# A four-layer linear/softmax attention kernel: side work of the first linear passes planned by steps, weights' preparation loosened, residuals and the attention's first rows asked for elsewhere

## The chip, the cores and the metric

The kernel runs on one core of one Trainium2 chip. The metric is the device time of one execution in microseconds; three runs are shown, and their median counts. One further execution was taken by the hardware profiler; all rows of the profile come from it.

## The reference, cut to what matters

Input x has 2048 rows of 512; 32 heads of 16. Four layers follow one another, A, B, A, B, each reading the layer norm of x and adding its result to x. Both A layers share their weights, and so do both B layers.

```
def _A_ref(x, wqkv, w_phi, wo):                # linear attention with a learned feature map
    q, k, v = split_heads(x @ wqkv)
    pq, pk = q @ w_phi, k @ w_phi              # per head, 16 x 16
    phi_q = concat(softmax(pq), softmax(-pq))  # 32 features a head
    phi_k = concat(softmax(pk), softmax(-pk))
    kv, z = phi_k^T v, sum over rows of phi_k
    o = phi_q kv / (phi_q z + 1e-6)
    return heads_joined(o) @ wo

def _B_ref(x, wq, wk, wv, wo, beta):           # 4 segments of 512 rows, causal softmax within each
    for s in range(4):
        a_dot = softmax(qs ks^T / 4 + mask) vs
        a_mem = phi(qs) M / (phi(qs) z + 1e-6)         # phi(t) = t + 1 if t > 0, else exp(t)
        out_s = sigmoid(beta) * a_mem + (1 - sigmoid(beta)) * a_dot
        M, z = M + phi(ks)^T vs, z + sum phi(ks)
    return joined(out) @ wo

x = x + _A_ref(layernorm(x), ...)
x = x + _B_ref(layernorm(x), ...)
x = x + _A_ref(layernorm(x), ...)
x = x + _B_ref(layernorm(x), ...)
```

## The kernel before, in words

**Tiles.** The 2048 rows are 16 tiles of 128 (`NT`) in four segments of four. A 512-wide weight is held as high and low part (`hi`, `lo`), and each projection of a tile is twelve matmuls of 128x512 (`mm3`: four chunks, three products each), made by a generator that yields after each three. All projections, transposes and sums share three PSUM buffers `g`; the key-value sums use `lg` and `mx`.

**Layer A, first pass** (`pass1`). It goes over the segments in the order `SEGS` = 1, 2, 3, 0. In each, `go` runs the steps k0 k1 q0 q1 k2 v0 k3 q2 q3: a k step projects a key tile (`kproj`), copies it on ACT, takes each head's extremes on DVE (`extremes`) and their differences on POOL (`differences`); `exp` on ACT and `scale_k` (sums on DVE, one half multiplied on DVE, one on POOL) follow one and two steps later. A q step projects a query tile (`qproj`), copies it, takes its extremes, and stores it to DRAM (`pqs`). Step v0 is `kv(0)`, the sum of keys times values over the first two tiles; `kv(1)`, over the last two, is put into the next segment as `late`, behind k0. Each yield of `go` is one step i; a segment has 34 to 36. Beside them, from i = 4 on, one step of a chain of generators `side` is made per i: first the last four steps of the next segment's norm (`columns`: transposes into `hT`), then `v_tile` for the next segment (16 steps), then eleven steps (`rows`) of the norm after that (`norm_T` with `slow`: load of four tiles; four steps of statistics on DVE; `root` on ACT; `refine` on POOL; four steps of `normal` on ACT). What is left of `side` at the segment's end is stepped through alone. The first segment of the second A layer has all four parts in `side`, since there the pass begins within the end of layer B.

**Weights' preparation** (`prepare`). In the first A layer it is run turn by turn with `pass1`: one yield of each. It loads B's and A's other weights in blocks, splits each piece into `hi` (a cast on ACT, tile `oh`) and `lo` (a subtraction on POOL, tile `ol`), and stores both to DRAM: 32 pieces of a quarter block for `wqk`, then twelve whole 128x512 pieces. There are three buffers each of `xr` (the load), `oh` and `ol`. One piece is taken every `EVERY` = 2 yields, after `PREP` = 6 more.

**The order on each engine.** A scheduler places the instructions, but each helper engine (`dve`, `act`, `pool`, `sync`) is wrapped in `Ordered`: every instruction is chained behind the one issued before it on its engine, so that program order holds there. `held` does the same for PE. A list put off until the end of layer B, `aside`, takes the work of the next pass's first key tiles (`features`) out of the way of B's last sums.

**Layer A, second pass** (`pass2`). For each tile i: transposes of its features (8), their product with the key-value sums (16 small matmuls), normalisation, transposes of the result of tile i - 1 (`turn`), and `out_proj` of tile i - 1 with its residual, which `residual` loads and `end` adds on DVE and stores. The residual of tile i is asked for after `out_proj` of tile i - 1. A tile is nine steps. The first `A20` = 82 steps run alone, but for the `opening` of layer B, which is stepped at some of them (two loads of `wqk`, four of `bwv`, eleven steps of the first segment's norm, four `fills` of constants). The rest is done within B's loop.

**Layer B** (`steps`). A loop over slots k from `BEGIN` = -31 runs the attention by a table; heads come in groups m, five slots each: `maxima` (products, then row maxima on DVE; slot 5m - 9 on, tile `mx`), `attend` (tile `lg`, exponentials on ACT, masks on POOL; slot 5m on), `weighted` (`pv`). `BEFORE` lists what the slots below zero do: at -30 to -27 the `columns` of the first segment (`ln0`), from -25 on the projections. The rest of pass 2 is spread over slots -9 to 1 by its PE work: each slot brings the total up to its share of `LEFT` = 40000 ns, and the last does what remains. The slots after that follow tables that the change does not touch, and at the end of the first B layer they step through the second A layer's `pass1` (`after`).

Of the kernel before, what the change touches and what calls it, by code (L numbers as in the profile page):

```python
# [34 lines left out]
LEAD = 9  # L35
FINAT = 8
PAUSE, DONE = object(), object()
LEFT = 40000
BEGIN = -31
MAXIMA = -9  # L40
A20 = 82
PREP = 6
EVERY = 2
NEXT = (3, 2, 3, 2)
SEGS = (1, 2, 3, 0)
# [51 lines left out]
6.1 max out~       | 6.3 fin           | 6.4 pt~  # L97
7.1 p pt~          | 7.3 fin p pt      | 7.4 p pt
"""
BEFORE = {-30: "ln0", -29: "ln0", -28: "ln0", -27: "ln0", -25: "q0", -23: "v0", -21: "k0", -20: "load", -19: "v1",  # L100
          -18: "n", -17: "v2 n", -16: "n", -15: "n n", -14: "q1 n", -13: "n", -12: "k1 n", -11: "n", -10: "v3 n",
          -4: "max q2~", -1: "t0"}

# [2 lines left out]
def interleave_kernel(ctx, tc, x_in, a_wqkv, a_wphi, a_wo, b_wq, b_wk, b_wv, b_wo, b_beta,  # L106
# [24 lines left out]

    last = [None]
    ends = {}
    put_off = [None]
    aside = [None]

# [12 lines left out]

    class Ordered:  # L150

        def __init__(self, engine):
            self.engine = engine

        def __getattr__(self, op):
            f = getattr(self.engine, op)

            def call(*a, **k):
                i = f(*a, **k)  # L159
                if self.engine in ends:  # L160
                    behind(i, ends[self.engine])
                ends[self.engine] = i
                return i
            return call

# [32 lines left out]
    def constants():  # L198

        sync.dma_start(out=mask, in_=c_mask)  # L200
        sync.dma_start(out=eb, in_=b_beta.unsqueeze(0).broadcast_to([P, H]))
        yield
        act.activation(eb, eb, AF.Exp, scale=-1.0)
        dve.tensor_scalar(eb, eb, 1.0, None, op0=ADD)
        dve.reciprocal(gates[:, 1, :], eb)
        dve.tensor_scalar(gates[:, 0, :], gates[:, 1, :], -1.0, 1.0, op0=MUL, op1=ADD)
        for j in range(4):
            dve.tensor_copy(share[32 * j : 32 * j + 32, :], gates[32 * j : 32 * j + 32, 0, j:H:4])
        dve.tensor_scalar(share, share, -1.0, bd[:, 24:25], op0=ADD, op1=MUL)
        dve.tensor_scalar(share, share, 1.0, None, op0=ADD)  # L210
        dve.tensor_copy(ones, bd[0:32, 25:26].broadcast_to([32, P]))
# [84 lines left out]
    def prepare():  # L296


        yield from constants()
        for _ in range(PREP):  # L300
            yield
        jobs = [(src, kc) for src in (b_wq, b_wk, a_wo, b_wv, b_wo) for kc in range(NC)]
        asked = []

        def rows():

            while jobs and len(asked) < 3:
                src, kc = jobs.pop(0)
                asked.append(T2("xr", 3))
                sync.dma_start(out=asked[-1], in_=src[kc * P : (kc + 1) * P, :])  # L310
            return asked.pop(0)

        def parts():
            return rows(), T2("oh", OO, F32R), T2("ol", OO, F32R)

        def pieces():
            for m in range(2):
                for kc in range(NC):
                    tiles = parts()
# [12 lines left out]

        copied, stored = None, None
        for piece in chain(pieces(), (None, None)):
            if stored:
                _, keep, tiles = stored
                for k, t in zip(keep, tiles):
                    dma(k, t.rearrange("p (c x) -> p c x", c=NC) if len(k.shape) == 3 else t)
            if copied:
                (raw, hi, lo), _, _ = copied  # L340
                pool.tensor_tensor(out=lo, in0=raw, in1=hi.bitcast(F32), op=SUB)
            if piece:
                (raw, hi, _), _, _ = piece
                act.copy(hi, raw)
            copied, stored = piece, copied
            for _ in range(EVERY):
                yield
# [166 lines left out]
    def chain(*gens):  # L514
        for g in gens:
            yield from g
# [56 lines left out]
    class LayerA:  # L573
# [68 lines left out]
        def pass1(self, first):  # L642
# [5 lines left out]
                spare = ("e8" if first else "w8") if n % 2 else None  # L648
                return h, norm_T(self.xsrc, SEGS[n], h, spare, slow=True, off=True)

            def rows(g):
                for _ in range(11):
                    next(g)
                    yield

            if first:
                wq, wk, wv, upc = self.first(hTs, vv, upcoming)
            else:
# [16 lines left out]
            for n, s in enumerate(SEGS):  # L675
# [55 lines left out]
                if n < NSEG - 1:  # L731
                    if n == 0 and not first:
                        upc = upcoming(1)
                        next(upc[1])
                    hTs, g = upc
                    vv = []
                    side = [] if n or first else [rows(g)]
                    side += [g, v_tile(hTs, wv, vv, ("g", G))]
                    if n + 2 < NSEG:
                        upc = upcoming(n + 2)  # L740
                        side.append(rows(upc[1]))
                    side = chain(*side)
                    e = {}

                    def go(late):

                        ready, done = [], []
                        for step in "k0 k1 q0 q1 k2 v0 k3 q2 q3".split():
                            if step == "v0":
                                yield from kv(0)  # L750
                                continue
                            t = int(step[1])
                            yield from (kproj if step[0] == "k" else qproj)(t, e)
                            if done:
                                es.append(scale_k(e[done.pop()]))
                            if ready:
                                exp(e[ready[0]])
                                done.append(ready.pop())
                            if step[0] == "k":
                                ready.append(t)  # L760
                            if step == "k0" and late:
                                yield from late

                    for i, _ in enumerate(go(late)):
                        if i == 4 and n == 0 and not first:
                            wq = load_w("awq", None, "e8")
                        if aside[0] is None and i > 3:
                            next(side, None)
                        if n == 1 and i % 4 == 0:
                            settle(1)  # L770
                        yield
                    for _ in side:
                        yield
                    late = kv(1)
                    continue

# [35 lines left out]
        def pass2(self):  # L812
# [4 lines left out]
            for i in range(NT + 1):  # L817
# [15 lines left out]
                if i < NT:  # L833
# [13 lines left out]
                    if i + 3 < NT:  # L847
                        self.e[i + 3] = differences(*self.raw.pop(i + 3))
                    self.load_q(i + 4)
                if i > 0:  # L850
                    yield from out_proj(x, self.xdst, i - 1, oT, self.wo)
                if i < NT:
                    x = residual(self.xsrc, i, ("ot", OT))


    class LayerB:
# [271 lines left out]
        def opening(self):  # L1128
            self.w4 = []
            self.wnext = [(m, c) for _ in range(NSEG) for c in range(NC) for m in range(2)]  # L1130
            for _ in range(2):
                self.queue_w()
                yield
            self.wv = []
            yield from bring(self.wv, "bwv")
            self.norm0 = self.norm(0)
            next(self.norm0)
            fills = self.start()
            for n in (0, 0, 1, 1, 1, 1, 1, 1, 0, 1, 1, 1, 1):
                yield  # L1140
                next(fills, None)
                for _ in range(n):
                    next(self.norm0)

        def steps(self, side, after, table_end):

# [134 lines left out]
    for i in range(2):  # L1281
# [3 lines left out]
        opening = lb.opening()  # L1285
        for k in range(A20):
            next(a2)
            if k % 3 == 0 and (5 < k < 24 or k > 41):
                next(opening, None)
        for _ in opening:  # L1290
            pass
# [32 lines left out]
```

## Time and profile before

| | us |
|---|---|
| median of three runs | 1654.8 |
| runs | 1653.51, 1654.8, 1656.23 |
| profiled execution, own time | 1648.24 |
| its span, first to last instruction | 1646.1 |
| mean granted TensorE clock | 0.972 |

In the profile PE is TensorE's matmuls, PEld its weight loads, DVE VectorE, ACT ScalarE, POOL GpSimd, SP the queue that issues the DMAs. A row of a wait reads: who waited, for whom, total us, times, longest. A row of a stretch reads: from and to, length, then busy us and instructions of PE, PEld, DVE, ACT and POOL, the granted clock, the DMA engines' share and GB/s. A row of a timeline reads: start, duration, engine, operation, written tile and read tiles, size, number; in brackets the idle time before it and what ended that. L159 and L180 are the helpers through which nearly all instructions go, so tiles tell them apart: `tb` is the copy of a query tile, `U` of a key tile, `P` the features, `x` rows being normalised, `st` their statistics, `oh` and `ol` the parts of a prepared weight (or of a turned result), `xr` and `ot` residuals (`xr` also a weight's load).

The stages of the span: the first A layer's first pass until about 235 us, its second pass until 296 with a rest until 381, B until about 850 with the second A layer's start inside, the second A layer's first pass until about 1038, its second pass until 1098 with a rest until 1183, and B.

### The profile page before, as it was taken

The page shows a single profiled execution, that of the slowest core. Times are in us where ns is not written, and L with a number is a line of the kernel's source. Part 1 is how long each engine was busy: PE and PEld are TensorE (multiplying, and loading weights), DVE is VectorE, ACT ScalarE, POOL GpSimd, SP SyncE. Part 2 cuts the span into 40 slices and gives each one's busy share as a digit, 9 for nine tenths or more (in the row PEclk, how much of TensorE's full clock was granted, in tenths as well). Part 3 has the DMA queues.
Part 4 walks back from the last instruction along what each step waited for, and adds up shares of the span by engine and source line. Part 5 has one row for each costly group of instructions (what it writes and reads, how often), then busy time and mean ns, then how long its engine had stood idle before and what let it go on. Part 6 is the DMA issues. An engine that isn't in the chain of part 4 may idle for free.

```text
span 1646.1 us, 28161 instructions
## 1 busy us (share of the span) xinstructions
PE 1532.6 (93%) x9856; PEld 1095.2 (67%) x9856; DVE 1130.5 (69%) x3252; ACT 787.4 (48%) x1178; POOL 652.4 (40%) x1006
## 2 busy tenths in 40 slices
PE   7978899998899999999998989999889999999998
PEld 6766687775566666666567778877656666666554
DVE  5544377486887877888644456666777778777784
ACT  5334334434656556556532333344355655654553
POOL 1445474322444444433222235543134445533422
PEclk9978999999999999999997989999999999999999
DMA  4265537434533533534241102455344444343331
GB/s 157 84 230 159 177 99 220 147 114 116 169 97 97 155 94 106 144 97 109 89 164 45 39 26 65 157 156 174 113 127 123 117 116 134 86 135 92 91 76 60
DMA packets 108763, 195.69 MB, mean 119 GB/s; under 512 B 14416, under 2 KB 27856, under 8 KB 107856
## 3 DMA queue, kind: packets, MB, share of 16 engines
q1 hardware_dynamic: 107472, 193.38, 39.9%
q8 instruction: 79, 1.29, 0.3%
q10 hardware_dynamic: 1152, 0.52, 0.1%
q14 instruction: 60, 0.49, 0.1%
HBM read 101.05 MB, written 39.85 MB: 86 GB/s over the span
## 4 chain that ended last, share of the span: by engine, by line
PE 64%; DVE 19%; issue 5%; ACT 5%; POOL 3%; DMA 2%; SPq 1%; ACTq 0%; POOLq 0%; DVEq 0%
PE g L180 36%; DVE mx L159 8%; PE mx L180 8%; PE lg L180 7%; PE pv L180 6%; PE g L184 6%; POOL P L159 2%; DVE es L159 2%; ACT P L159 2%; ACT tb L159 2%; DVE mxs L159 1%; DVE bs L159 1%; DVE mmq L159 1%; DVE ta L159 1%; DMA ot<-in 1%
## 5 line engine op out<-in xcount | busy, mean ns | idle before, releaser
L159 DVE CUSTOM_DVE_ANT_0 mx<-mx,mask 128x128 f32<-128x128 f32 (+3 forms) x1024 | 510.9, 499 | 163.7 <-PE mx L180 129.2
L159 ACT ACTIVATE P<-lg 128x1024 f32<-128x1024 f32 x320 | 328.8, 1028 | 185.4 <-PE lg L180 173.1
L159 POOL TENSOR_SCALAR_AFFINE_SELECT P<-P 128x256 f32<-128x256 f32 (+1 forms) x448 | 191.3, 442 | 438.2 <-ACT P L159 436.8
L180 PE MATMUL g<-hh,wqk 128*128 128x512 f32 x512 | 182.5, 411 | 2.4 <-ACT hh L159 1.7
L180 PE MATMUL mx<-e,e 63*128 63x256 f32 (+2 forms) x1024 | 155.6, 361 | 23.0 <-DVE mxs L159 17.2
L180 PE MATMUL lg<-e,e 64*128 64x256 f32 (+2 forms) x1024 | 168.7, 387 | 8.0 <-ACT P L159 7.1
L180 PE MATMUL g<-w,oh 128*128 128x512 f32 x512 | 168.4, 410 | 2.5 <-ACT oh L159 2.1
L180 PE MATMUL pv<-P,v 128*32 128x512 f32 (+3 forms) x2048 | 164.9, 441 | 0.0
L180 PEld LDWEIGHTS lg<-e,e 64*128 64x128 f32 x1024 | 81.4, 185 | 103.8 <-issue 53.6
L180 PE MATMUL g<-w,hh 128*128 128x512 f32 x448 | 146.6, 408 | 1.2 <-ACT tb L159 0.9
L159 DVE DVE_READ_ACCUMULATOR2_ANT mxs<- 128x1 f32 x1024 | 144.9, 142 | 0.0
L180 PEld LDWEIGHTS mx<-e,e 63*128 63x128 f32 x1024 | 83.5, 186 | 71.2 <-DVE mxs L159 52.3
L180 PEld LDWEIGHTS pv<-P,v 128*32 128x32 f32 x2048 | 53.6, 109 | 98.2 <-issue 88.2
L180 PEld LDWEIGHTS g<-hh,wqk 128*128 128x128 f32 x512 | 98.2, 192 | 24.3 <-ACT hh L159 2.1
L180 PEld LDWEIGHTS g<-w,oh 128*128 128x128 f32 x512 | 89.2, 188 | 23.9 <-ACT oh L159 3.5
L159 POOL TENSOR_SCALAR tb<-tb 128x512 f32<-128x512 f32 x48 | 71.5, 1491 | 84.2 <-ACT tb L159 84.2
L180 PE MATMUL g<-w,ol 128*128 128x512 f32 x256 | 101.3, 396 | 1.4 <-DVE ol L159 1.4
L180 PE MATMUL g<-hl,wqk 128*128 128x512 f32 x256 | 101.7, 397 | 0.2
L159 ACT CAST ta<-g 128x512 fp32r<-128x512 f32 x64 | 37.5, 585 | 122.1 <-PE g L180 122.1
L180 PEld LDWEIGHTS g<-w,hh 128*128 128x128 f32 x448 | 79.7, 190 | 20.4 <-ACT tb L159 3.1
L159 DVE TENSOR_REDUCE mmq<-tb 128x32 f32<-128x512 f32 x64 | 40.9, 680 | 72.1 <-ACT tb L159 72.1
L159 POOL TENSOR_TENSOR P<-P,es 128x512 f32<-128x512 f32 x32 | 49.1, 1533 | 102.4 <-DVE es L159 102.1
(133 smaller groups left out, 2794.3 us busy)
## 6 DMA issues: line engine op xcount, KB each, us to landing
e<-ta SPq DMA_DIRECT2D x384, 128.0 KB
wqk<-wqk SPq DMA_DIRECT2D x64, 512.0 KB
x<-x SPq DMA_DIRECT2D x48, 256.0 KB
xr<-in SPq DMA_DIRECT2D x28, 256.0 KB
pq<-tb SPq DMA_DIRECT2D x24, 256.0 KB
tb<-pq SPq DMA_DIRECT2D x24, 256.0 KB
x<-xr SPq DMA_DIRECT2D x24, 256.0 KB
xr<-x SPq DMA_DIRECT2D x24, 256.0 KB
```

The costliest lines, as they stand in the source:

```text
L159: i = f(*a, **k)
L180: return held(nc.tensor.matmul(*a, **k))
L184: return held(nc.tensor.transpose(*a))
```

## The change

Constants: `LEFT` 40000 to 25000, `BEGIN` -31 to -25, `A20` 82 to 105, `PREP` 6 to 3 (with one more yield within `constants`).

In `pass1` the chain `side` is replaced by `plan`, a list of pairs of a step and a generator: at step i every entry due is made. In the ordinary segments `columns` stay at steps 4 to 7, the sixteen steps of `v_tile` lie from 10 to 34, and the eleven of the later norm at 8, 14, 16, 18, 20, 22, 24, 28, 30, 32, 34, among them. In the second A layer's first segment the first norm's remaining steps lie at 8 to 20, four of them (the statistics) being appended to `aside`; `v_tile` lies from 21 to 33, and the later norm from 21 to 36. What is due after the end is made without yields. `late` goes behind k1 instead of k0.

`Ordered` gets a flag `loose`: instructions issued under it are still placed behind the last chained one of their engine, but later ones are not chained behind them. `prepare` issues all its casts, subtractions, loads and stores under it.

In `pass2` the residual of tile i is asked for before `out_proj` of tile i - 1. The `opening` has the whole norm of the first segment, fifteen steps with its `columns`, spread with the `fills` over steps of pass 2, and `BEFORE` loses its four `ln0`.

```
-LEFT = 40000
-BEGIN = -31
+LEFT = 25000
+BEGIN = -25
-A20 = 82
-PREP = 6
+A20 = 105
+PREP = 3
-BEFORE = {-30: "ln0", -29: "ln0", -28: "ln0", -27: "ln0", -25: "q0", ...
+BEFORE = {-25: "q0", ...
...
                 if self.engine in ends:
                     behind(i, ends[self.engine])
-                ends[self.engine] = i
+                if not loose[0]:
+                    ends[self.engine] = i
...  # prepare
-        copied, stored = None, None
-        for piece in chain(pieces(), (None, None)):
+        def turn_by_turn():
+            loose[0] = True
+            piece = next(todo, None)
+            loose[0] = False
+            return piece
+
+        copied, stored, todo = None, None, pieces()
+        for piece in chain(iter(turn_by_turn, None), (None, None)):
+            loose[0] = True
             if stored:
...
+            loose[0] = False
             copied, stored = piece, copied
             for _ in range(EVERY):
                 yield
...  # pass1
-                    side = [] if n or first else [rows(g)]
-                    side += [g, v_tile(hTs, wv, vv, ("g", G))]
+                    if n or first:
+                        plan = [(4 + j, g) for j in range(4)]
+                        vals, norms = [10 + j * 26 // 16 for j in range(16)], (8, 14, 16, 18, 20, 22, 24, 28, 30, 32, 34)
+                    else:
+                        plan = [(j, g) for j in (8, 9, 12, 13, 14, 15, 17, 18, 19, 20)]
+                        vals, norms = [21 + j * 13 // 16 for j in range(16)], (21, 26, 27, 28, 29, 30, 31, 33, 34, 35, 36)
+                    vt = v_tile(hTs, wv, vv, ("g", G))
+                    plan += [(j, vt) for j in vals]
                     if n + 2 < NSEG:
                         upc = upcoming(n + 2)
-                        side.append(rows(upc[1]))
-                    side = chain(*side)
+                        plan += [(j, upc[1]) for j in norms]
+                    plan.sort(key=lambda x: x[0])
...
-                            if step == "k0" and late:
+                            if step == "k1" and late:
                                 yield from late
...
                         if i == 4 and n == 0 and not first:
                             wq = load_w("awq", None, "e8")
-                        if aside[0] is None and i > 3:
-                            next(side, None)
+                            aside[0].append(lambda: [next(g) for _ in range(4)])
+                        while plan and plan[0][0] <= i:
+                            next(plan.pop(0)[1], None)
...
-                    for _ in side:
-                        yield
+                    for _, step in plan:
+                        next(step, None)
...  # pass2
                     self.load_q(i + 4)
+                    ahead = residual(self.xsrc, i, ("ot", OT))
                 if i > 0:
                     yield from out_proj(x, self.xdst, i - 1, oT, self.wo)
-                if i < NT:
-                    x = residual(self.xsrc, i, ("ot", OT))
+                x = ahead
...  # opening
-            for n in (0, 0, 1, 1, 1, 1, 1, 1, 0, 1, 1, 1, 1):
-                yield
-                next(fills, None)
-                for _ in range(n):
-                    next(self.norm0)
+            for n in (0, 0, 1, 0, 1, 0, 1, 0, 1, 1, 1, 0, 1, 1, 1, 1, 1, 1, 1, 1):
+                yield
+                next(self.norm0 if n else fills, None)
...
         for k in range(A20):
             next(a2)
-            if k % 3 == 0 and (5 < k < 24 or k > 41):
+            if k in (6, 9, 12, 18, 24, 30) or k > 41 and k % 3 == 0:
                 next(opening, None)
```

More of the change, by code (lines that the diff above doesn't have):

```diff
@@ L99 @@
 """
-BEFORE = {-30: "ln0", -29: "ln0", -28: "ln0", -27: "ln0", -25: "q0", -23: "v0", -21: "k0", -20: "load", -19: "v1",
+BEFORE = {-25: "q0", -23: "v0", -21: "k0", -20: "load", -19: "v1",
           -18: "n", -17: "v2 n", -16: "n", -15: "n n", -14: "q1 n", -13: "n", -12: "k1 n", -11: "n", -10: "v3 n",
@@ L133, in interleave_kernel @@
     ends = {}
+    loose = [False]
     put_off = [None]
@@ L649, in upcoming @@
                 return h, norm_T(self.xsrc, SEGS[n], h, spare, slow=True, off=True)
-            def rows(g):
-                for _ in range(11):
-                    next(g)
-                    yield
             if first:
```

## The prediction

> **What bounds the kernel now.** I read the page first, then TensorE's waits, then the stretches of the span with their granted clock, then the timelines of the stretches where PE stands.
>
> ```profile
> span 1646.1 us, 28161 instructions
> PE 1532.6 (93%) x9856; PEld 1095.2 (67%) x9856; DVE 1130.5 (69%) x3252; ACT 787.4 (48%) x1178; POOL 652.4 (40%) x1006
> PEclk9978999999999999999997989999999999999999
> ```
>
> PE is busy 93% and no other engine over 69%. So 113 us of PE's idle time, and whatever the clock takes, is all that an edit of order alone can return. The clock's digit falls below 9 in two places, the two linear layers' first passes.
>
> ```profile
> PE mx L180 <- POOL P L159: 27.4, 9, 8.9
> PE g L184 <- ACT x L159: 9.9, 2, 5.9
> PE g L180 <- ACT tb L159: 6.0, 4, 4.8
> PE g L184 <- DVE ot L159: 4.5, 4, 1.5
> ```
>
> The first row is the key-value sum `kv`, which waits for POOL's half of `scale_k`. The second is `columns`, which waits for ACT's normalised rows. The fourth is pass 2. The next rows place them (PE, PEld, DVE, ACT, POOL busy, then granted clock).
>
> ```profile
> 44.00:82.00 38.00, 35.88 (x168) 28.33 (x166) 20.63 (x34) 13.69 (x29) 17.07 (x22) 1.00 0.29 91
> 82.00:104.00 22.00, 12.22 (x53) 11.36 (x54) 7.42 (x11) 7.27 (x15) 9.89 (x19) 0.53 0.71 257
> 104.00:140.00 36.00, 35.84 (x174) 29.51 (x171) 16.60 (x29) 14.30 (x30) 17.97 (x26) 1.00 0.51 173
> 140.00:160.00 20.00, 11.98 (x56) 11.16 (x57) 11.24 (x16) 8.54 (x16) 11.15 (x13) 0.66 0.52 162
> 160.00:180.00 20.00, 17.77 (x75) 13.46 (x73) 5.66 (x9) 6.89 (x11) 9.84 (x8) 1.00 0.49 148
> 180.00:190.00 10.00, 6.56 (x26) 5.50 (x26) 3.65 (x5) 2.21 (x4) 3.66 (x3) 0.66 0.47 166
> 240.00:296.00 56.00, 52.05 (x342) 44.04 (x340) 39.64 (x86) 25.77 (x41) 26.00 (x30) 1.00 0.65 202
> 296.00:308.00 12.00, 9.64 (x39) 7.24 (x40) 4.36 (x9) 2.94 (x5) 3.40 (x5) 0.86 0.09 20
> 325.00:381.00 56.00, 53.07 (x324) 42.00 (x323) 43.87 (x127) 20.14 (x33) 14.69 (x15) 1.00 0.44 129
> 860.00:884.00 24.00, 15.79 (x67) 14.04 (x66) 11.25 (x17) 6.13 (x10) 6.69 (x12) 0.64 0.03 11
> 905.00:917.00 12.00, 8.07 (x42) 7.57 (x42) 5.00 (x10) 5.15 (x10) 3.64 (x10) 0.72 0.00 0
> 953.00:971.00 18.00, 11.56 (x51) 10.49 (x50) 9.75 (x14) 4.58 (x9) 5.50 (x6) 0.62 0.08 29
> 1042.00:1098.00 56.00, 53.12 (x350) 44.90 (x348) 39.85 (x86) 26.46 (x42) 26.16 (x31) 1.00 0.64 202
> 1098.00:1110.00 12.00, 9.31 (x38) 6.95 (x39) 4.68 (x10) 3.04 (x6) 3.40 (x5) 0.86 0.07 15
> ```
>
> Row 104:140 is a projection pass with `v_tile` woven in evenly: PE idles 0.16 us of 36 at full clock, no other engine reaches half. That is the floor. Where the clock is below 1.00, PE stood before; its loss in a stretch is about busy time x (1 - clock).
>
> **First linear layer, 44 to 190.** Idle by the rows: 2.1 + 9.8 + 0.2 + 8.0 + 2.2 + 3.4 = 25.7 us. Clock: 12.22 x 0.47 + 11.98 x 0.34 + 6.56 x 0.34 = 12.0 us. Together 37.7.
>
> Of this, the edits reach: the next segment's normalisation, now between steps 8 and 34 instead of after step 23 (statistics at least six steps after the load, refine four steps before the first normalised tile), so ACT's projection copies no longer queue behind a `normal` that waits for POOL; `kv(1)`, now behind k1 and not k0; and the weights' preparation, whose stores no longer queue on SP behind a load that waits for POOL. What `kv` waits for is this piece of the chain that ended last (start, duration), 5.3 us from the projection's copy on:
>
> ```profile
> 117.73 0.60 ACT tb L159
> 118.36 1.28 DVE mmq L159 x2
> 119.64 1.14 DVE es L159
> 120.80 0.56 DVE es L159
> 121.49 1.52 POOL P L159
> ```
>
> PE's own pace in these passes, from its timeline:
>
> ```profile
> 163.14 0.86 PE L180 MATMUL g<-w,e 128*128 128x512 f32 x3
> 164.53 0.86 PE L180 MATMUL g<-w,e 128*128 128x512 f32 x3
> ```
>
> The two rows stand six matmuls apart: 0.23 us a matmul. In the changed order `kv(1)` stands 27 matmuls and four sets of transposes behind the last q projection, over 7 us: covered. `kv(0)` stands 21 matmuls behind q1, 24 before, since `v_tile` is thinned to 16 steps in 26: 4.8 us against 5.3. That is a new wait of 0.5 us in each segment; nothing queues behind it but PE's own matmuls.
>
> The preparation keeps a risk:
>
> ```profile
> 182.13 0.62 ACT L159 CAST oh<-xr 128x512 fp32r<-128x512 f32 x1 [7.43 <-DMA bwv<-oh]
> ```
>
> ACT stood 7.43 us for a store to land, with q1's copy behind it and PE behind that copy. ACT still runs these casts in a fixed order. With stores issued earlier I take half of row 180:190 (idle 3.4 + clock 2.2) as staying, with bounds of nothing and of all rows from 140 on (20.0). Staying: 2.1 (first row) + 1.5 (`kv(0)`, three segments) + 2.8 + half of 160:180's 2.2 = 7.5. **Gain 30; bounds 14 and 36.**
>
> **Second linear layer, 860 to 971.** Idle 8.2 + 3.9 + 6.4 = 18.6, clock 15.79 x 0.36 + 8.07 x 0.28 + 11.56 x 0.38 = 12.3, together 30.9. The later two stretches are the same waits as above, without preparation beside them. The first is the start behind the attention:
>
> ```profile
> 853.50 2.46 DVE L159 TENSOR_REDUCE mm<-U 128x32 f32<-128x512 f32 x4
> 855.87 0.69 DVE L159 BATCH_NORM_STATS2 bs<-x 128x6 f32<-128x512 f32 x1
> 854.35 1.07 POOL L159 TENSOR_TENSOR P<-U,mm 128x512 f32<-128x512 f32 x1 [15.35 <-DVE mm L159]
> 863.88 0.48 POOL L159 TENSOR_TENSOR st<-st 128x4 f32<-128x4 f32 x2
> 865.57 1.52 ACT L159 ACTIVATE x<-x,st 128x512 f32<-128x512 f32 x2 [5.65 <-POOL st L159]
> 867.00 0.56 ACT L159 COPY tb<-g 128x512 f32<-128x512 f32 x1
> 866.44 1.12 PE L184 MATMUL g<-ident,x 128*128 128x128 f32 x4 [5.93 <-ACT x L159]
> 872.30 3.26 PE L180 MATMUL lg<-v,P 128*128 128x68 f32 x14 [2.28 <-POOL P L159]
> ```
>
> Here the edit helps little. The put-off list now runs the four statistics ahead of the second key tile's extremes. So DVE: first extremes until 854.75, statistics 3.4 until 858.2, second extremes until 859.5. POOL: two differences of 1.07 until 861, then refine (863.88 to 865.57 is 1.7), now ahead of `scale_k`, until 862.6. ACT: four rows of 0.76 until 865.6, then q1's copy until 866.2, after which the chain's remaining 4.7 us end at 870.9. PE has six matmuls of k2 before the first transposes (nine before), so stands from 859.8 to 863.4, passes three columns by 865.8, and stands 5.1 us for `kv(0)`: 8.7 us of waits against 5.93 + 2.28, though the sum starts 1.4 us earlier with one column more done. I keep 8.5 of idle and the 5.7 of clock, and 0.5 for `kv(0)` in two more segments: 15.2 stay. **Gain 16; bounds 8 (half of the later stretches returns) and 28.**
>
> **Pass 2 and the attention's opening, twice.**
>
> ```profile
> 252.19 0.69 DVE L159 TENSOR_TENSOR ot<-g,ot 128x512 f32<-128x512 f32 x1 [1.49 <-DMA ot<-in]
> 259.77 0.69 DVE L159 TENSOR_TENSOR ot<-g,ot 128x512 f32<-128x512 f32 x1 [1.84 <-DMA ot<-in]
> ```
>
> These two rows, a tile apart at 7.6 us, would be 5.7 apart without the wait: the residual's load stood on SP behind the store of the tile before. Now it stands ahead of it, one tile's time more. Idle in 240:296 is 4.0, in 1042:1098 2.9; I leave 1.5 each: **gain 4**. Rows 296:308 and 1098:1110 are the first rows' columns with nothing beside them: idle 2.4 and 2.7, clock 1.4 and 1.3. They now sit among tiles; 0.8 each stays: **gain 6**.
>
> Against that, A20 82 to 105 moves 23 steps, at nine steps a tile 2.6 tiles, out of 325:381, where they run beside the maxima, into pass 2 proper: 2.6 x 5.7 = 14.7 us added there. The 325:381 stretch is then shorter by that at most (PE 53.07 against DVE 43.87 leaves PE the bound), and by 9 if the maxima's DVE work, whose one buffer PE waits for, shows through. I take 12.5: **loss 4 over both layers; bounds 0 and 12**. BEGIN's six slots fewer held only the `ln0` steps that have moved. Both together: gain 6, bounds -8 and 13.
>
> **Sum.** 30 + 16 + 6 = 52. Span 1646.1 - 52 = 1594; the profiled execution took 1648.24, so 1596. The median shown, 1654.8, lies 6.6 above it; I take the same 52 off: **1603 us**.
>
> The Trainium skill ("TensorE: Matmul & The Clock Gate", Part 1, the HAM clock gate) says that the penalty of warming up is under 1% of a typical kernel's span, an estimate of at most 16 us here. The rows above give 12.0 + 12.3 + 2.7 = 27 us, so the trace disagrees; by that figure less clock could be returned and the time would be about 1611.
>
> **The rivals.**
> - *The wait moves (0.17).* `kv(0)` and the preparation take over: the first layer returns 14, the second 8, the opening nothing: 1633. For it: 5.3 against 4.8, and 865.57's example. Against: 104:140.
> - *The clock stays low (0.05).* Only idle returns. Of the 52, clock is 10.9 + 6.6 + 2.7 = 20: 1623. Against: every low row holds a stand. The Trainium skill's figure above lies between this and the forecast.
> - *Slower (0.07).* The preparation becomes the bound. The twelve whole 128x512 pieces now meet a faster pass; if each cast waits as at 182.13 and costs PE the 4.8 us of the waits' third row and 2.2 of clock, that is 12 x 7.0 = 84, less the 2.8 already counted: 1684. It decides from about eight of twelve on (52 / 7.0). Against: with the stores ahead of POOL's work, a piece's round is shorter than before.
> - *All stands go (0.06).* Bounds 36 + 28 + 13 = 77: 1578.
> - *No effect (0.03).* The scheduler restores the old order. Against: PE's new order does alternate `v_tile` over the whole segment.
>
> **How the numbers follow.** The forecast has 0.62. Its own bounds, without the extremes at once, give 1580 to 1628; to hold 8 in 10 I take in half of the first rival: 1580 to 1634. Some 0.2% (3.3 us) is about what a measurement of this kernel can tell from no change. Faster by more: 0.62 + 0.17 + 0.05 + 0.06 = 0.90; within: 0.03; slower: 0.07.
>
> **What would show it.** Right: the wait of `mx` for POOL falls from 27 to some 8 us; the granted clock of the first layer's pass is 1.00 but for one short dip; near the second layer's start `g<-ident,x` and the key-value sum still wait, some 8 us together; `ot` no longer waits for its load; the stretch of 325:381 is some 12 us shorter while pass 2 before it is 11 longer. Wrong: casts `oh` that wait over 5 us for stores with PE behind them; a `kv(0)` that waits 2 us or more in each segment; PE idle beside the maxima while DVE is full.

## The result, and the profile after

The changed kernel takes 1601.67 us (median of six runs, 1596.23 to 1604.31), the kernel before 1653.45 (median of six, the three shown ahead of the prediction among them; 1647.17 to 1656.23): ratio 0.9685, 95% interval 0.9661 to 0.9709, so 52 us less, 48 to 56. The profiled execution of after took 1604.31 us, 43.9 less than that of before (1648.24). The two measures differ because the profiled execution of before lies 5.2 under the median of its runs, and that of after 2.6 over its own. Everything read from the two traces below must therefore add up to 44, not to 52.

The page of after, three lines; TensorE's clock digit is below 9 in three of forty slices, and 8 in each:

```profile
span 1602.6 us, 28186 instructions
PE 1518.1 (95%) x9856; PEld 1083.3 (68%) x9856; DVE 1130.9 (71%) x3252; ACT 785.6 (49%) x1178; POOL 651.7 (41%) x1006
PEclk9998999999999999999988999999999999999999
```

TensorE's waits in after (who, for whom, total us, times, longest):

```profile
PE lg L183 <- POOL P L161: 6.3, 5, 4.1
PE g L187 <- ACT x L161: 4.1, 1, 4.1
PE g L187 <- DVE w L161: 2.9, 2, 2.0
PE mx L183 <- POOL P L161: 1.3, 2, 0.7
```

The 27.4 us of `mx` have become 1.3. Those of `lg`, the other tile of the key-value sums, rose from 2.4 to 6.3, of which one wait is 4.1. The wait for the normalised rows `x` is one of 4.1. No row for `ot` is left. Helper lines 159, 180 and 184 are now 161, 183 and 187.

The stretches of after that answer to those shown of before (same columns):

```profile
82.00:104.00 22.00, 21.21 (x122) 18.18 (x120) 15.45 (x27) 9.68 (x23) 13.54 (x18) 1.00 0.99 367
104.00:140.00 36.00, 34.44 (x184) 28.87 (x184) 15.98 (x25) 18.22 (x34) 24.81 (x32) 1.00 0.57 180
140.00:160.00 20.00, 15.34 (x65) 13.28 (x64) 8.85 (x13) 5.59 (x10) 12.67 (x10) 0.75 0.74 268
160.00:180.00 20.00, 20.00 (x87) 16.20 (x87) 10.40 (x16) 5.96 (x9) 6.67 (x6) 0.99 0.27 70
830.00:850.00 20.00, 13.74 (x56) 11.99 (x56) 10.78 (x17) 7.18 (x11) 7.77 (x14) 0.57 0.26 79
850.00:882.00 32.00, 29.44 (x132) 23.23 (x130) 15.54 (x28) 11.73 (x21) 8.43 (x12) 0.95 0.12 36
882.00:960.00 78.00, 75.98 (x399) 63.99 (x399) 42.71 (x66) 24.98 (x40) 25.20 (x30) 1.00 0.08 30
```

One bad stretch is left in each first pass. Their rows in the timeline of after, and behind them the two rows that the next table uses as marks (the first product of features and key-value sums, where each second pass starts) and one wait of a column:

```profile
145.64 0.62 ACT L161 CAST oh<-xr 128x512 fp32r<-128x512 f32 x1 [3.62 <-DMA bwv<-ol]
146.17 0.58 ACT L161 COPY tb<-g 128x512 f32<-128x512 f32 x1
151.48 1.76 PE L183 MATMUL lg<-v,P 128*128 128x68 f32 x7 [4.09 <-POOL P L161]
834.16 1.11 PE L187 MATMUL g<-ident,x 128*128 128x128 f32 x4 [4.12 <-ACT x L161]
841.09 1.12 PE L187 MATMUL g<-ident,x 128*128 128x128 f32 x4 [1.96 <-DVE w L161]
879.64 0.66 PE L187 MATMUL g<-ident,x 128*128 128x128 f32 x4 [1.59 <-DVE hl L161]
208.12 0.66 PE L183 MATMUL g<-KN,P 128*128 128x68 f32 x4 [0.33 <-ACT P L161]
996.31 0.66 PE L183 MATMUL g<-KN,P 128*128 128x68 f32 x4 [0.33 <-ACT P L161]
```

In the first layer one cast of the preparation waits 3.62 us for a store to land, q1's copy stands behind it, and 5 us later the key-value sum stands 4.09. In the second layer the columns stand 4.12 for their normalised rows and 1.96 for DVE. The same marks in the timeline of before:

```profile
236.73 0.66 PE L180 MATMUL g<-KN,P 128*128 128x68 f32 x4 [0.33 <-ACT P L159]
1039.81 0.66 PE L180 MATMUL g<-KN,P 128*128 128x68 f32 x4 [0.33 <-ACT P L159]
```

The matmuls between any two marks are the same in number, so the span can be cut into six stages: (1) from the start to the first of those marks; (2) the next 1400 matmuls, which hold the second pass, the attention's opening and a part of B that is the same in all kernels; (3) on to the last product for the maxima of the first B, the same in all; (4) on to the second mark, the second linear layer's first pass; (5) 1400 matmuls again; (6) on to the last matmul, the same in all. The stages are in us, from one trace each; each ratio is to runs of the kernel before that were taken beside that kernel's, so ratios compare better than medians:

| kernel | median | ratio to before (95%) | 1 | 2 | 3 | 4 | 5 | 6 |
|---|---|---|---|---|---|---|---|---|
| before | 1653.45 | 1 | 236.7 | 234.4 | 341.2 | 227.4 | 233.7 | 368.8 |
| after | 1601.67 | 0.9685 (0.9661-0.9709) | 208.1 | 231.9 | 341.2 | 215.1 | 231.9 | 370.2 |
| e1_plan_alone | 1625.96 | 0.9834 (0.9809-0.9859) | 222.6 | 235.5 | 341.1 | 214.7 | 236.9 | 370.3 |
| e2_prep_chained | 1613.97 | 0.9770 (0.9746-0.9794) | 221.4 | 229.6 | 341.2 | 214.0 | 231.5 | 368.8 |
| e3_old_second_pass | 1611.15 | 0.9752 (0.9727-0.9777) | 202.4 | 237.2 | 341.1 | 214.3 | 233.5 | 368.8 |
| e4_old_residual | 1608.48 | 0.9741 (0.9715-0.9766) | 206.5 | 235.3 | 341.1 | 214.5 | 233.7 | 368.7 |
| e5_late_k0 | 1619.48 | 0.9788 (0.9759-0.9816) | 213.6 | 229.7 | 341.0 | 226.7 | 231.5 | 370.2 |
| e6_stats_early | 1596.35 | 0.9656 (0.9628-0.9683) | 206.4 | 232.1 | 341.2 | 211.4 | 230.5 | 368.7 |
| e6b_root_early | 1598.85 | 0.9664 (0.9639-0.9688) | 206.4 | 230.2 | 341.1 | 211.1 | 232.1 | 370.1 |
| e7_even_prep | 1592.38 | 0.9629 (0.9602-0.9657) | 200.4 | 233.6 | 341.0 | 213.4 | 229.2 | 368.9 |
| f1_both | 1588.72 | 0.9630 (0.9602-0.9659) | 200.1 | 231.4 | 341.1 | 211.0 | 229.2 | 370.2 |
| f2_dense_late | 1589.96 | 0.9630 (0.9601-0.9659) | 200.9 | 229.2 | 341.1 | 209.8 | 233.5 | 370.4 |
| f3_a20_95 | 1589.08 | 0.9625 (0.9596-0.9654) | 201.5 | 229.3 | 341.0 | 209.9 | 230.2 | 370.3 |
| f4_old_opening | 1604.30 | 0.9720 (0.9688-0.9752) | 206.4 | 232.0 | 341.3 | 214.3 | 232.8 | 370.5 |

Between the two profiled executions the change took 28.6 us from stage 1, 2.5 from 2, nothing from 3, 12.3 from 4, 1.8 from 5, and stage 6 was 1.4 longer. How far one trace can be trusted the table shows too, since many kernels share a stage's code:

- Stage 6 is the same everywhere and lies between 368.7 and 370.5.
- Stage 1 is the same in after, e3, e4, e6, e6b and f4: 202.4 to 208.1, four of them at 206.4 or 206.5.
- Stage 4 is the same in after, e2, e3, e4, e7 and f4: 213.4 to 215.1, mean 214.3.
- Stages 2 and 5 together are the same in after, e2, e5, e6, e6b, e7, f1 and f2: 460.6 to 463.8, mean 462.1. With the old second pass and opening (before, e1, e3) they take 468.1 to 472.4, mean 470.4.

In stage 1, in stage 4 and in the sum of 2 and 5 the trace of after is the longest of its code, so what is read from before and after alone comes out too small.

### The profile page after: what moved, and what is told of

It reads as the page before. It is cut to its first block, busy times and chain, and to the rows that moved or that the text cites. A ratio compares the mean times of both kernels' runs of the same rounds, so it can differ in the third digit from the quotient of the medians.

```text
span 1602.6 us, 28186 instructions
## 1 busy us (share of the span) xinstructions
PE 1518.1 (95%) x9856; PEld 1083.3 (68%) x9856; DVE 1130.9 (71%) x3252; ACT 785.6 (49%) x1178; POOL 651.7 (41%) x1006
## 4 chain that ended last, share of the span: by engine, by line
PE 67%; DVE 18%; ACT 5%; issue 5%; POOL 3%; DMA 2%; SPq 0%; ACTq 0%; POOLq 0%; DVEq 0%
PE g L183 38%; DVE mx L161 8%; PE lg L183 8%; PE mx L183 8%; PE g L187 7%; PE pv L183 7%; POOL P L161 2%; ACT tb L161 2%; DVE es L161 2%; ACT P L161 1%; DVE mxs L161 1%; DVE ta L161 1%; DVE mmq L161 1%; ACT x L161 1%; DMA xr<-in 1%
## 5 line engine op out<-in xcount | busy, mean ns | idle before, releaser
L161 ACT COPY v<-g 128x512 f32<-128x512 f32 x64 | 37.6, 587 | 120.1 <-PE g L183 119.8
L183 PE MATMUL g<-w,hl 128*128 128x512 f32 x224 | 88.1, 393 | 0.0
```

The costliest lines, as they stand in the source:

```text
L183: return held(nc.tensor.matmul(*a, **k))
```

## Experiments

**Which edit holds the first layer.** The theory was that plan and preparation share it; the rivals gave it to one of them. e1 is before with only the first pass changed:

```
-                    side = [] if n or first else [rows(g)]
...
+                        vals, norms = [10 + j * 26 // 16 for j in range(16)], (8, 14, 16, ...)
...
-                            if step == "k0" and late:
+                            if step == "k1" and late:
```

> The kernel before with the changed first pass alone (plan by steps, key-value sum behind k1); preparation, second pass and opening as before. Theory (the plan takes the stands, the preparation keeps its own): the second layer's first pass returns its 13, the first layer's returns 14 to 18 of 28, since the stands from 140 us on in the trace of before lie beside the preparation: 27 to 31 less than before, about 1625. Rival 1 (the preparation's chained stores held the first layer): the first layer returns under 8, in all under 21, 1632 or more. Rival 2 (the loose chain is worth nothing): the first layer returns 25 or more, in all 38 or more, 1615 or less.

Measured 1625.96. Stage 1 is 14.1 us shorter than before, stage 4 12.7: the theory's numbers. e2 is after with the preparation of before:

```
-            loose[0] = True        # turn_by_turn and the loop over pieces
...
-PREP = 3
+PREP = 6
```

> The changed kernel with the preparation of before: every cast, subtraction, load and store chained in program order again, six yields ahead of it. Theory: the first layer's pass is 10 to 14 us longer than in the changed kernel (164 us between its marks), with PE waiting for casts or for key-value sums behind them after 120 us; 1612 to 1616. Rival 1: 20 us longer or more, 1622 or more. Rival 2: within 3 us of the changed kernel.

Measured 1613.97; stage 1 is 13.3 us longer than after's and within 1.2 of e1's. ACT and TensorE in the timeline of e2:

```profile
131.83 0.62 ACT L161 CAST oh<-xr 128x512 fp32r<-128x512 f32 x1 [6.17 <-DMA wqk<-oh]
144.88 0.62 ACT L161 CAST oh<-xr 128x512 fp32r<-128x512 f32 x1 [6.27 <-DMA awo<-oh]
147.72 0.58 ACT L161 COPY tb<-g 128x512 f32<-128x512 f32 x1
148.35 1.22 PE L183 MATMUL g<-w,e 128*128 128x512 f32 x2 [6.75 <-ACT tb L161]
158.68 0.62 ACT L161 CAST oh<-xr 128x512 fp32r<-128x512 f32 x1 [7.07 <-DMA bwv<-oh]
164.52 0.70 PE L183 MATMUL lg<-v,P 128*128 128x68 f32 x2 [7.25 <-POOL P L161]
```

Three casts wait 6.17, 6.27 and 7.07 us for stores, and PE stands 6.75 and 7.25 behind the later two. Loosened, the same pass holds one such wait of 3.62. Why the stores were late, SP shows. First its waits for POOL's subtractions between 100 and 200 us of e2, and two of its rows:

```profile
SPq L161 <- POOL ol L161: 33.9, 11, 5.5
140.66 0.33 SPq L161 DMA_DIRECT2D xr<-in  x1
141.04 0.43 SPq L161 DMA_DIRECT2D awo<-oh  x1
```

Then the same waits in after, with one cast and its store:

```profile
SPq L161 <- POOL ol L161: 11.5, 5, 4.6
131.27 0.62 ACT L161 CAST oh<-xr 128x512 fp32r<-128x512 f32 x1 [2.87 <-DMA xr<-in]
131.91 0.32 SPq L161 DMA_DIRECT2D awo<-oh  x1
```

In e2 the piece cast at 131.83 is stored at 141.04, behind a load that waited for POOL; in after the store follows its cast by 0.02 us. That is the reason that the forecast gave for this edit.

So the plan alone returns 14.1 us of stage 1 and the preparation on top of it 14.5, about half each, and each clears its own waits. The preparation without the plan was not run, and e2 puts `PREP` back together with the chain, so their shares are not known apart.

**What carries the plan.** The prediction named two reasons for the key-value sum's waits: ACT's copies queued behind a `normal` that waits for POOL, and the sum's place. e5 is after with the old place alone:

```
-                            if step == "k1" and late:
+                            if step == "k0" and late:
```

> The changed kernel with the second key-value sum of a segment put behind the next segment's k0 again, not behind k1. Theory: behind k0 only twelve matmuls (2.8 us) and two sets of transposes cover the 5.3 us of its chain, so it waits 2 to 2.5 us in two segments of each layer, 8 to 10 us of PE's idle time, and some 4 us of clock behind the longer ones: 1610 to 1616; PE waits for POOL's half of the features at tile mx again. Rival (the 27 us of those waits came from ACT's queue, which the plan cleared, and the place behind k1 is worth nothing): within 2 us of the changed kernel.

Measured 1619.48, somewhat past the theory's end: stage 4 is 11.6 us longer than after's, within 0.7 of before's, and stage 1 5.5 longer. The timeline of e5:

```profile
873.73 0.82 ACT L161 ACTIVATE x<-x,st 128x512 f32<-128x512 f32 x1 [1.02 <-POOL st L161]
874.45 0.56 ACT L161 COPY tb<-g 128x512 f32<-128x512 f32 x1
879.75 2.62 PE L183 MATMUL mx<-v,P 128*128 128x68 f32 x11 [4.71 <-POOL P L161]
```

And the same place in the timeline of after:

```profile
872.76 0.82 ACT L161 ACTIVATE x<-x,st 128x512 f32<-128x512 f32 x1 [1.03 <-POOL st L161]
873.49 0.56 ACT L161 COPY tb<-g 128x512 f32<-128x512 f32 x1
877.16 1.58 POOL L161 TENSOR_TENSOR P<-P,es 128x512 f32<-128x512 f32 x1 [4.43 <-DVE es L161]
881.26 1.45 PE L183 MATMUL mx<-v,P 128*128 128x68 f32 x12
```

ACT's queue is the same in both: q3's copy stands behind a normalised row that waits 1.0 us for POOL. In after POOL is done at 878.7 and the sum starts at 881.3, so the chain is covered, not shorter. With the plan there, the second layer gains nothing without the new place, and the first about a fifth less. The place without the plan was not run.

**The second pass.** e3 has the second pass and the opening of before, e4 only the residual's old place, f4 only the old opening:

```
-LEFT = 25000            # e3, f4; also BEGIN, A20, BEFORE, opening
+LEFT = 40000
...
-                    ahead = residual(self.xsrc, i, ("ot", OT))    # e3, e4
...
+                if i < NT:
+                    x = residual(self.xsrc, i, ("ot", OT))
```

> The changed kernel with the second pass and the attention's opening of before: residuals asked for late, the first rows' columns at slots -30 to -27, 82 steps alone, 40000 of work left for the maxima. Theory (both gain 6 together in the forecast, some 3 between the two traces): 3 to 6 us slower, 1605 to 1608; from the second pass's start to the first maxima 88 us again and not 97, beside the maxima 60 and not 50. Rival (what the columns gain is lost by tiles that leave the cover of the maxima, and by the two short stretches of half clock beside them that the changed kernel shows): the same time or up to 3 us faster.

> The changed kernel with only the residual asked for behind the projection again. Theory: PE's idle time in each second pass rises from 3.0 to some 5 us, 2 us a layer, 4 in all: 1605 to 1606, and DVE's sums wait for the residual's load again. Rival (three buffers of PSUM hide that wait from PE): DVE waits, PE does not, the time stays within 1 us.

> The changed kernel with the attention's opening of before (columns at slots -30 to -27, 82 steps alone, 40000 left) but the residual asked for ahead of the projection. Theory (between the runs without either and without the residual's place alone there were 0 to 3 us): 0 to 3 us slower than the changed kernel, 1602 to 1605; the second pass loses its waits for residuals, and keeps 2.4 us of idle time at the columns. Rival 1 (the forecast's terms: columns 6, tiles 4): 2 us. Rival 2 (the tiles out of the maxima's cover cost more than the columns give): 1 to 4 us faster.

Measured 1611.15, 1608.48 and 1604.30: e3 and e4 lie 2 to 3 us above their theories' ranges, f4 within its own. Stages 2 and 5 together are longer than after's by 6.9 in e3, by 5.2 in e4 and by 1.0 in f4, and than the mean of after's code by 8.6, 6.9 and 2.7. So the residual's place is worth 5 to 7 us, and the columns among the tiles gain 1 to 3 us more than the tiles lose that left the maxima; the smaller of these is within what single traces of one code differ by. The stretches are nearly as said: from the second pass's start to the first product for the maxima 97.1 us in after, 88.1 in before, 85.4 in f4; from there to the same matmul behind the maxima 49.9, 60.2 and 60.2. The residual's wait, in the timeline of e4:

```profile
221.45 0.69 DVE L161 TENSOR_TENSOR ot<-g,ot 128x512 f32<-128x512 f32 x1 [1.00 <-DMA ot<-in]
234.52 0.69 DVE L161 TENSOR_TENSOR xr<-g,xr 128x512 f32<-128x512 f32 x1 [1.30 <-DMA xr<-in]
235.27 0.66 PE L187 MATMUL g<-ident,tmp 128*128 128x128 f32 x4 [0.94 <-DVE xr L161]
```

PE's idle time in e4 is 1.6 us above after's in stage 2 and 3.1 in stage 5, 4.7 in all (2 to 4.5 above the other traces of after's code). The clock adds nothing over the two stages: e4 has one short stretch of half clock more in stage 2, behind a wait that after has too without the fall, and one less in stage 5.

**What is left: the start of the second layer.** e6 takes the four statistics before B's last sums:

```
-plan = [(j, g) for j in (8, 9, 12, 13, 14, 15, 17, 18, 19, 20)]
+plan = [(j, g) for j in (4, 5, 6, 7, 8, 9, 12, 13, 14, 15, 17, 18, 19, 20)]
...
-aside[0].append(lambda: [next(g) for _ in range(4)])
```

> The changed kernel with the four statistics at the second layer's start taken at steps 4 to 7 in program order, where DVE has gaps of 2 to 3 us ahead of B's last sums, and not from the put-off list. Theory: POOL's refine and ACT's normalised rows come 2 to 3 us earlier; PE's 4.1 us for them become 1 to 1.5, the 2.0 behind them goes, and with the stand part of the 20 us at 0.57: 4 to 8 us faster, 1594 to 1598, all of it in the stretch of the second layer's first pass (210 us between its marks). Rival (the statistics wait for their rows' load or hold up B's last sums on DVE): PE stands in front of those sums instead, the same time or up to 3 us slower.

Measured 1596.35, in the theory's range; stage 4 is 3.7 us shorter, though the ratio's interval overlaps after's. The timeline of e6:

```profile
828.33 0.66 PE L187 MATMUL g<-ident,x 128*128 128x128 f32 x4 [1.17 <-ACT x L161]
830.93 0.66 PE L187 MATMUL g<-ident,x 128*128 128x128 f32 x4 [1.25 <-ACT tb L161]
835.28 1.12 PE L187 MATMUL g<-ident,x 128*128 128x128 f32 x4 [3.00 <-DVE w L161]
```

The wait for `x` fell from 4.12 to 1.17 as expected, but most of it came back: 1.25 behind q1's copy and 3.00 for DVE, where 1.96 stood. PE's idle time in stage 4 fell by only 0.8 us; the rest of the 3.7 is clock, at half for 13.7 us there against after's 23.9. e6b has the rest of the norm earlier (steps 4, 5, 6, 7, 7, 7, 8, 9, 12, 13, 17 to 20):

> As the run before, with ACT's root and POOL's refine at step 7 too and the first two normalised rows at steps 8 and 9. Theory: the whole norm is ready when the second key tile's matmuls end: PE's waits for x and w are gone, 6 to 10 us faster than the changed kernel, 1592 to 1596. Rival (ACT's root waits for DVE's statistics with the copy of the second key tile queued behind it): the wait moves to that copy, the extremes come 1 to 2 us later and the key-value sum stands instead; no better than the run before.

A miss: 1598.85, stage 4 at 211.1 against e6's 211.4. The wait for `x` is gone; 1.34 and 3.79 us stand in its place, for q1's copy and for DVE. As the rival had it, this is no better than e6, but the stand is at the columns and not at the key-value sum.

**What is left: the preparation.** e7 evens out the pace of the pieces:

```
-            for _ in range(EVERY):
+            for _ in range(1 if n < 32 else 4):
```

> The changed kernel with the preparation's pace evened out: one step a quarter piece and four steps a whole piece, in place of two each, so each block of 256 KB gets four steps or more. Theory (the whole pieces came faster than their stores land, which is the one long stand left in the first layer: 4.1 us and the half clock behind it): that stand goes, 3 to 8 us faster in the first layer's pass, 1594 to 1599. Rival (the quarter pieces at twice the pace crowd ACT and POOL in the first 60 us of it): new stands there, the same time or up to 6 us slower.

Measured 1592.38, better than the theory's range; stage 1 is 7.7 us shorter than after's, 6 shorter than the usual 206.4 of that code and 2 shorter than its shortest. The stretches of e7:

```profile
104.00:140.00 36.00, 34.46 (x189) 29.21 (x189) 18.58 (x29) 17.84 (x31) 22.22 (x26) 1.00 0.64 231
140.00:160.00 20.00, 19.63 (x102) 16.53 (x101) 8.85 (x13) 4.02 (x7) 7.40 (x7) 1.00 0.17 62
```

The clock stays at 1.00 and PE idles 0.4 us of the 20 where after idled 4.7; the quarter pieces at twice the pace cost nothing that the trace shows. The last cast starts at 132 us, in after at 153, so the whole pieces also lie beside earlier work; pace and place were not tried apart.

**Together, and three more edits.**

> The changed kernel with the statistics at steps 4 to 7 and with the preparation's even pace together. Theory (the two waits lie in different layers and add): 3 to 5 us less than with the even pace alone, ratio to the kernel before 0.958 to 0.961, about 1587; first layer's pass 155 us and second layer's 207 between their marks. Rival (each only removes clock that the other's run lost by chance): no better than 0.963.

f1 (e6 and e7) takes 1588.72: stages 1 and 4 are 200.1 and 211.0, so the parts add in the stages; against e7, stage 4 has 2.9 us less of PE's idle time. But the ratio is 0.9630, that of e7 alone (0.9629) and not the theory's 0.958 to 0.961, so the time does not show the second part: by the time, the rival stands.

f2 adds to f1:

```
+vals = [(2 if late else 0) + j for j in (8, 10, 12, 14, 16, 17, 18, 19, 22, 24, ...)]
+plan = [(j, g) for j in (4, 5, 6, 7, 8, 9, 16, 16, 16, 16, 17, 18, 22, 23)]
```

> The run before with two more edits. In the ordinary segments four steps of the next values lie beside k2, so 24 matmuls and not 21 stand ahead of the first key-value sum; theory (5.3 us of chain against 4.8 of cover in the forecast): its waits of 0.7 us in the middle segments go. At the second layer's start the four normalised rows come behind q1's copy on ACT and two of the four columns behind the first key-value sum; theory: that sum's chain is 3 to 4 us shorter, PE stands 3 us less in front of it. Together 3 to 8 us less than the run before, about 1581. Rival (PE has no other work there, so a shorter chain for the sum leaves the columns and the values behind them late): the same wait at the columns or at the values' copies, within 2 us of the run before.

A miss; the rival holds. Time unchanged (1589.96), stage 4 1.2 us shorter. Of the five short waits of key-value sums that f1 has in the middle segments three are gone; one stays in each layer, 0.85 and 0.68. The timeline of f2:

```profile
825.55 0.69 PE L183 MATMUL lg<-v,P 128*128 128x68 f32 x2 [3.05 <-POOL P L161]
878.63 0.59 ACT L161 COPY tb<-g 128x512 f32<-128x512 f32 x1 [0.15 <-PE g L183]
879.49 0.66 DVE L161 BATCH_NORM_STATS2 bs<-x 128x6 f32<-128x512 f32 x1
880.28 1.25 DVE L161 TENSOR_REDUCE mmq<-tb 128x32 f32<-128x512 f32 x2
884.95 1.22 PE L183 MATMUL lg<-v,P 128*128 128x68 f32 x9 [0.68 <-POOL P L161]
```

At the start the stand only moved from the columns to the sum (3.05). In the later segment the sum still waits 0.68 with 24 matmuls ahead of it: q1's extremes, ready at 879.2, start at 880.28 behind the next norm's statistics on DVE. So by this trace the statistics' place, not only the count of matmuls, makes that wait; moving them was not tried.

f3 adds `A20 = 95` and `LEFT = 31500`:

> The run before with ten steps of the second pass moved back beside the maxima: 95 steps alone, 31500 of work left. Theory (beside the maxima PE stands 5.4 us and not 4.0, with two short stretches of half clock, since it has too little of its own there): 1 us of idle time and one or two such stretches of 1.5 us return per layer, 1 to 5 us less than the run before. Rival (DVE's maxima are covered at either size): within 1 us; the second pass is 6 us shorter before the maxima and the stretch beside them 6 us longer.

Inconclusive, as the rival had it: 1589.08. From the second pass's start to the maxima 90.0 us, beside them 54.1: the one gives what the other takes.

f1, f2 and f3 are faster than before and than the changed kernel by a further 9 (from the ratios) to 13 us (from the medians), and cannot be told apart. f1 is the simplest of them.

## Why the prediction was right, and where it was not

The forecast was 1603; the median is 1601.67. Faster was right, and no rival came about. Its sum of 52 fits the medians' 51.8; the two traces give 44, since that of after is the longest of its code in three places. Over all traces of the same code the change takes 30 us from stage 1, 13 from stage 4 and 8 from stages 2 and 5, where 30, 16 and 6 were forecast. One term is 3 too large and another 2 too small, so that the total is so close is in part luck.

- **First layer: 30 forecast, 28.6 between the traces,** about 30 by the 206.4 that most kernels with this code show. Left over were key-value sums of 0.40 and 0.79 us where 0.5 each was said, 1.56 at a segment's columns, and one cast behind a store. The sum behind that cast stood 4.09 us and the clock was 0.75 for 20 us, some 8 us where the forecast kept 2.8. The 2.1 us kept for the first row shrank to 0.7.
- **Second layer: 16 forecast, 12.3 measured, 13 over all traces: the term that was too large.** Its start cost what was kept, 13.5 us against 8.5 + 5.7 = 14.2, but by two errors that cancel. PE waits 4.12 + 1.96, 6.1 in all and not 8.5: the key-value sum there does not wait at all, where 5.1 was forecast, and the 1.96 is for DVE, which takes the low part of a transposed column only behind q1's extremes and sums. The clock takes more, 13.74 x 0.43 + 29.44 x 0.05 = 7.4 and not 5.7. The two later sums wait 0.68 and 0.38, as said. What the sum left out are the columns at the next segments' starts, which now wait 0.97, 1.59 and 0.96 us, 3.5 in all (the 1.59 is shown above).
- **The two reasons were not weighed.** "ACT's projection copies no longer queue behind a `normal` that waits for POOL" holds in three of four places: such a row waited 5.39 and 1.47 us in the first layer of before, 1.77 and 1.78 in the second, and in after one wait of 1.03 is left, with q3's copy behind it. But e5 has the same queue and returns nothing in the second layer. What the sum lacked there was cover, and the place behind k1 gives it.
- **Second pass and opening: 6 forecast, 4.3 between the two traces, 8 over all.** The residual gives up to 4.7 us of idle time by e4 (4 said). Columns and tiles give 1 to 3 by f4, where 6 - 4 = 2 was said. The moved tiles did nearly what was said: 9.0 us longer before the maxima and 10.3 shorter beside them (11 and 12 said). PE's idle time beside the maxima rose from 4.0 to 5.5.
- **The slower rival** needed eight of twelve whole pieces to hold up PE. One did. e2 shows that the danger was real in the old chain, and e7 that a better pace removes it.
- **The clock.** Its mean rose from 0.972 to 0.983, and to 0.991 in e7. The Trainium skill's figure ("TensorE: Matmul & The Clock Gate", Part 1), weighed in the forecast, gave 1611; the runs, 1596 to 1604, all lie below that. The page gives the figure for the ramp to full clock, not for falls in mid kernel, so the 27 us do not contradict it as the forecast said.

## What to carry to other kernels

When a sum waits for the last piece of a chain over three engines, first try to put it behind more of its own engine's work; here, with the queue in front of the chain cleared already, one line still decided a whole layer's gain. Pace background work by bytes and not by pieces: with four steps for a piece of four times the size, which also moved the pieces earlier, no cast waited for a store any more. Check a forecast against stages that hold identical code, since they show how far a single trace may be off.

## What was not expected of the hardware

Low clock follows short stands only in some executions. The same 6.8 us near the end, in after:

```profile
1569.90:1573.30 3.40, 2.22 (x15) 1.24 (x13) 0.68 (x2) 2.48 (x4) 2.21 (x5) 1.00 0.02 4
1573.40:1576.80 3.40, 3.40 (x19) 1.31 (x20) 0.56 (x1) 1.40 (x3) 0.46 (x2) 0.50 0.00 0
```

and in before:

```profile
1615.30:1618.70 3.40, 2.22 (x15) 1.24 (x13) 0.68 (x2) 2.48 (x4) 2.20 (x5) 1.00 0.02 5
1618.80:1622.20 3.40, 3.40 (x26) 2.02 (x27) 0.56 (x1) 2.13 (x3) 0.86 (x3) 1.00 0.00 0
```

PE idles 1.18 us of 3.40 in both, in stands of at most 0.7 us; in after the clock is then halved for 3.4 us (19 matmuls in place of 26), in before not. This is stage 6's 370 against 368.8. Within one trace all stretches of half clock start whole multiples of 3.413 us apart (in after at 150.01 and 1573.37, which is 417 of them). In after one such window, from 1569.95 to 1573.37, holds all these stands, 1.16 us idle; in before a window starts at 1615.57, between them, and holds 0.97. The Trainium skill ("TensorE: Matmul & The Clock Gate", Part 1) describes a free-running window of 3413 ns; the spacing agrees with it, and it would explain why the same stand counts in one execution and not in another. Its section "Why this matters for your kernels" warns of idle gaps of about 3 us; here far shorter stands that add up to a third of a window were followed by half clock. No sharp limit comes out of the 14 traces: behind full clock and after the first matmuls, no window with under 0.77 us idle was followed by half clock and every one with over 2 was, but of those between, 51 were followed by it and 323 were not. What decides there is open.
